# One fused kernel of gated linear attention, mixture of experts and GLU: token numbers in 64-byte lines, less and earlier zeroing, routing cut into four steps

## The chip, the cores and the metric

The kernel runs on one core of a Trainium2 chip. The metric is the device time of one execution in microseconds (us). A core has a matrix engine (PE, TensorE; PEld is its loading of stationary operands), a vector engine (DVE), a scalar engine (ACT), a general engine (POOL, GpSimd) and SP, which here issues most DMAs. Each engine works through its own instructions in order. [...]

## The reference

Three layers follow one another, 3072 tokens (4 batches of 768) of width 384 (8 heads of 48).

```python
# 1. gated linear attention, per batch and head
f = 1 / (1 + exp(-f_logit))
for t in range(768):
    state = f[t][:, None] * state + outer(k[t], v[t])
    y[t] = q[t] @ state
x = y laid out as [3072, 384]
# 2. mixture of 8 experts, each token to its best one
logits = x @ w_gate;  e = argmax(logits);  gate = softmax(logits)[e]
out = gate * sigmoid(x @ w_output_gate)[e] * (relu(x @ w1[e]) @ w2[e])
# 3. gated linear unit, width 1536
result = (sigmoid(out @ wg) * (out @ wv)) @ wo
```

## The kernel before, in words

**The recurrence** takes the tokens in 24 units of 128 (4 batches of 6). A loop over i (lines 711 to 756) is written out in the order in which each engine is to work, with several units in flight. In iteration i, PE forms the scores of unit i (`s_score`, tile pS), then the output of unit i-1 (`s_y`, tile pY), the state's product of unit i (`s_state`, pM), the turned keys of unit i+1 (`s_turn`, pk), the turned output of unit i-1 (`s_rows`, px) and its router logits (`s_logit`, plg). ACT does the exponentials and logarithms (gi, ls, ln) and copies out of PSUM (xT, kt, x); `s_logit` and `s_rows` both need xT, which ACT copies from pY. DVE forms kT, masks the scores (am), makes running sums (ls) and updates the state (sn); POOL forms qT. SP issues the loads of all inputs, in order: ft, qk, v per unit.

**Routing** goes by groups of units; `groups` lists the first unit and the number of units. When the last unit of a group has its logits, a generator `route` is appended, and `step_route` runs its next step once per iteration, behind `s_sum` and ahead of `s_y` (from i = 17 on once more at the end). The lists `first` and `factor` in `choose` hold small instructions of DVE and one each of ACT: `ex` (exponential of the logits, in `first`) and `eg` (exponential of the output gate, in `factor`). `pr` counts on PE how many tokens of each expert come before each token; from it comes the slot `sidx`. Each expert has 512 slots of 386 words in `xs_all` in DRAM: 384 values of a token, its number (stored as 3072 minus the number, so that 0 means none) and its factor. `put_rows` sends a routed unit's rows to their slots: POOL copies the two extra words into the row, and then issues an indirect DMA.

**Zeroing.** Slots that may stay empty are zeroed ahead of the puts: at i = 2 to 9 SP sends 3 blocks of 128 slots per expert (`xs_all<-zrow`, 579 KB each). At i = 16 it zeroes `id_all` (14 KB). The put DMAs wait for the zeroing.

**The experts.** 9 passes follow: expert 0 in two (W0 = 208 tokens and then 288), the other seven by falling count, with 512, 456, 432, 424, 408, 392 and 376 tokens. `gather_rows` loads a pass's rows, `to_xt` turns them, and products with split weights (each weight as a high and a low part, three matmuls for one) go through `mm3`, lines 780 to 782. `feed` loads the weights (SP) and splits them into parts (ACT `w_hi`, DVE `w_lo`), for expert 0 within the recurrence, from i = 5 on one split per iteration. `put_ids` (line 464) writes the numbers of a pass's tokens from the gathered rows to `id_all`, so that the results find their places later. In the same stretch `conv` loads the GLU's weights as 64-bit words into `stg` (POOL's DMA queue, two buffers), and ACT, POOL and DVE turn them into 32-bit floats (`single`, from line 180).

**The GLU** takes 6 groups of 512 tokens; rows go to their places by indirect DMAs with the numbers read from `id_all` (line 971).

A check at the end of the plan compares counts with the sizes laid out; where it fails, a general version runs instead.

## Time and profile before

| what | value |
|---|---|
| median of 3 runs | 879.57 us (876.7 to 880.75) |
| the profiled execution | 882.84 us, of which its span is 881.1 us |
| PE busy | 847.5 us (96%), mean granted clock 0.978 |
| DVE, ACT, POOL busy | 458.5, 350.2, 204.2 us |
| DMA | 88.96 MB in 52750 packets, 12954 of them under 512 B |
| recurrence | about 10 to 158 us of the span |
| passes of the experts | about 158 to 425 us |
| GLU | about 425 to 881 us |

The span is one execution on the core, from its first to its last instruction. PE's busy time holds its slow time too: a matmul at half the clock counts double. So the time that PE lost in a stretch is its idle time and, beside it, the time in which it worked at the lower clock.

### The profile page before, as it was taken

The page shows a single profiled execution, that of the slowest core. Times are in us where ns is not written, and L with a number is a line of the kernel's source. Part 1 is how long each engine was busy: PE and PEld are TensorE (multiplying, and loading weights), DVE is VectorE, ACT ScalarE, POOL GpSimd, SP SyncE. Part 2 cuts the span into 40 slices and gives each one's busy share as a digit, 9 for nine tenths or more (in the row PEclk, how much of TensorE's full clock was granted, in tenths as well). Part 3 has the DMA queues.
Part 4 walks back from the last instruction along what each step waited for, and adds up shares of the span by engine and source line. Part 5 has one row for each costly group of instructions (what it writes and reads, how often), then busy time and mean ns, then how long its engine had stood idle before and what let it go on. Part 6 is the DMA issues. An engine that isn't in the chain of part 4 may idle for free.

```text
span 881.1 us, 14091 instructions
## 1 busy us (share of the span) xinstructions
PE 847.5 (96%) x5388; PEld 752.0 (85%) x5388; DVE 458.5 (52%) x866; ACT 350.2 (40%) x690; POOL 204.2 (23%) x201
## 2 busy tenths in 40 slices
PE   8998889999999999898999999999999999999995
PEld 5887778898899999898888888888888888888885
DVE  7775785557989998788454222222322322232221
ACT  7765674255456546543433212121221221122111
POOL 5215165302544454455200100010010001001001
PEclk9988898999999999999999999999999999999998
DMA  8998462488898988864300110020020001000001
GB/s 194 270 304 255 120 187 70 91 234 218 187 185 206 244 161 230 237 127 62 117 1 1 37 36 1 1 73 1 1 64 8 1 1 37 1 0 36 1 1 39
DMA packets 52750, 88.96 MB, mean 101 GB/s; under 512 B 12954, under 2 KB 33858, under 8 KB 52674
## 3 DMA queue, kind: packets, MB, share of 16 engines
q1 hardware_dynamic: 46050, 64.35, 29.8%
q0 software_dynamic: 6624, 23.62, 9.7%
q8 instruction: 44, 0.72, 0.4%
q14 instruction: 32, 0.26, 0.1%
HBM read 68.35 MB, written 19.60 MB: 100 GB/s over the span
## 4 chain that ended last, share of the span: by engine, by line
issue 49%; PE 23%; DMA 5%; DVE 4%; POOL 2%; ACT 1%; POOLq 0%; ACTq 0%; DVEq 0%
PE po L781 3%; PE ph L780 3%; PE po L780 3%; PE po L782 3%; PE ph L781 3%; PE ph L782 3%; DMA stg<-in_moe_w_out_dram 2%; POOL out_dram L991 2%; DMA stg<-in_moe_w_gate_dram 1%; DMA stg<-in_moe_w_val_dram 1%; DVE w_lo L232 1%; PE ptx L414 1%; PE pY L631 1%; PE pY L639 1%; PE plg L487 1%
## 5 line engine op out<-in xcount | busy, mean ns | idle before, releaser
L1119 DVE TENSOR_TENSOR hf<-pv,sg 128x512 f32<-128x512 f32 x72 | 49.8, 691 | 268.0 <-PE pv L782 264.0
L991 POOL DMA_INDIRECT out_dram<-ob,ids x24 | 23.6, 982 | 404.2 <-DVE ob L990 398.7
L1115 ACT ACTIVATE sg<-pg 128x512 f32<-128x512 f32 x72 | 43.0, 598 | 173.2 <-PE pg L782 173.2
L1122 ACT CAST hh<-hf 128x512 fp32r<-128x512 f32 x72 | 44.7, 621 | 159.5 <-DVE hf L1119 148.3
L232 DVE TENSOR_TENSOR w_lo<-st,w_hi 128x384 fp32r<-128x384 f32 (+1 forms) x112 | 95.5, 882 | 9.1 <-ACT w_hi L231 8.8
L781 PE MATMUL po<-w_lo,hh 128*128 128x384 f32 x288 | 96.6, 335 | 0.0
L780 PE MATMUL po<-w_hi,hh 128*128 128x384 f32 x288 | 96.4, 335 | 0.0
L782 PE MATMUL po<-w_hi,hl 128*128 128x384 f32 x288 | 96.3, 334 | 0.0
L781 PE MATMUL pv<-xt_lo,w_hi 128*128 128x512 f32 x216 | 85.5, 396 | 0.0
L782 PE MATMUL pg<-xt_hi,w_lo 128*128 128x512 f32 x216 | 85.5, 396 | 0.0
L780 PE MATMUL pg<-xt_hi,w_hi 128*128 128x512 f32 x216 | 85.5, 396 | 0.0
L780 PE MATMUL pv<-xt_hi,w_hi 128*128 128x512 f32 x216 | 85.1, 394 | 0.0
L781 PE MATMUL pg<-xt_lo,w_hi 128*128 128x512 f32 x216 | 85.1, 394 | 0.0
L782 PE MATMUL pv<-xt_hi,w_lo 128*128 128x512 f32 x216 | 85.1, 394 | 0.0
L781 PE MATMUL po<-hl,w_hi 128*128 128x208 f32 (+8 forms) x216 | 74.4, 344 | 3.6 <-DVE hl L1042 3.6
L780 PE MATMUL po<-hh,w_hi 128*128 128x208 f32 (+8 forms) x216 | 74.6, 345 | 1.4 <-ACT yt L951 1.4
L1123 DVE TENSOR_TENSOR hl<-hf,hh 128x512 fp32r<-128x512 f32 x72 | 49.9, 693 | 49.4 <-ACT hh L1122 49.4
L782 PE MATMUL po<-hh,w_lo 128*128 128x208 f32 (+8 forms) x216 | 74.3, 344 | 0.0
L780 PE MATMUL ph<-xt_hi,w_hi 128*128 128x288 f32 (+7 forms) x192 | 68.4, 356 | 2.6 <-DVE hl L1042 2.2
L181 POOL TENSOR_SCALAR cva<-cva 128x512 f32<-128x512 f32 (+1 forms) x30 | 57.2, 1907 | 55.6 <-ACT cva L180 55.6
L781 PE MATMUL ph<-xt_lo,w_hi 128*128 128x288 f32 (+7 forms) x192 | 67.5, 352 | 0.1
L782 PE MATMUL ph<-xt_hi,w_lo 128*128 128x288 f32 (+7 forms) x192 | 67.4, 351 | 0.0
(179 smaller groups left out, 1682.5 us busy)
## 6 DMA issues: line engine op xcount, KB each, us to landing
st<-in_moe_w_dram SPq DMA_DIRECT2D x48, 256.0 KB
st<-in_moe_w_dram SPq DMA_DIRECT2D x32, 384.0 KB
qk<-in_qkt_dram SPq DMA_DIRECT2D x48, 192.0 KB
xs_all<-zrow SPq DMA_DIRECT2D x8, 579.0 KB
ft<-in_ft_dram SPq DMA_DIRECT2D x48, 96.0 KB
v<-in_v_dram SPq DMA_DIRECT2D x24, 192.0 KB
stg<-in_moe_w_gate_dram POOLq DMA_DIRECT2D x9, 512.0 KB
stg<-in_moe_w_val_dram POOLq DMA_DIRECT2D x9, 512.0 KB
```

The source lines that it names most:

```text
L181: nc.gpsimd.tensor_scalar(out=af, in0=af, scalar1=HW_LEAST, scalar2=HW_MOST, op0=ALU.max, op1=ALU.min)
L232: nc.vector.tensor_tensor(out=lo, in0=src, in1=hi.bitcast(F32), op=ALU.subtract)
L414: nc.tensor.transpose(pts[kk][:, i * P : i * P + z], rows[0:z, i, kk * P : (kk + 1) * P], ident[0:z, 0:z])
L487: nc.tensor.matmul(pl, lhsT=d["xT"][:, hp, :], rhs=wgp[:, hp, :], start=(hp == 0), stop=(hp == HP - 1))
L780: nc.tensor.matmul(ps, lhsT=ah, rhs=bh, start=first, stop=False)
L781: nc.tensor.matmul(ps, lhsT=ah, rhs=bl, start=False, stop=False)
L782: nc.tensor.matmul(ps, lhsT=al, rhs=bh, start=False, stop=last)
L991: put = nc.gpsimd.indirect_dma_start(out=out[:, :], out_offset=bass.IndirectOffsetOnAxis(ap=idx[g][:, i : i + 1], axis=0), in_=ob, in_offs ...
L1115: nc.scalar.activation(out=sg, in_=pg, func=AF.Sigmoid)
L1119: nc.vector.tensor_tensor(out=hf, in0=pv, in1=sg, op=ALU.mult)
L1122: nc.scalar.copy(hh, hf)
L1123: nc.vector.tensor_tensor(out=hl, in0=hf, in1=hh.bitcast(F32), op=ALU.subtract)
```

## The change

- The rows of `id_all` become 16 words wide. `put_ids` writes the last 16 words of a gathered row (64 bytes: 14 values, the number, the factor) instead of the number alone (4 bytes); the number is then read at word 14. The zeroing of `id_all` goes.
- Slots are zeroed from the 257th of each expert on (it was the 129th): 2 blocks instead of 3, for two experts per iteration at i = 2 to 5. The first weights of expert 0 are issued at i = 6 (it was 3), their splits begin at i = 8 (it was 5). The check asks for 256 tokens of each expert (it was 128).
- `ex` moves from `first` to the head of `factor`. A route now has the steps: `first`; `ex`, product and sum of the output gate; then `pr`, `eg` and the rank; then, for the groups below unit 12, the rest in a step of its own.
- The third and fourth groups are (12, 5) and (17, 5) instead of (12, 6) and (18, 4); EARLY is 17; W0 is 192, so expert 0's passes have 192 and 304 tokens.
- The router's weights are loaded ahead of the first gates' work. In the experts' loop the last route is run to its end at i = 2, and the first step of the plan with it.

```diff
--- before.py
+++ after.py
@@ -63,13 +63,18 @@
     CAPS = (496, 512, 456, 432, 424, 408, 392, 376)
 
     XW = DM + 2
-    EARLY = 18
+
+    IW = 16
+    ID0 = XW - IW
+    EARLY = 17
 
     SOON = 12
 
     LATE = 19
 
-    W0 = 208
+    W0 = 192
+
+    LEAST = 256
 
     PD = P // 2 + D
     NRING = 34
@@ -89,7 +94,8 @@
     x_all = drp.tile([NT, DM], F32, name="x_all")
     xs_all = drp.tile([NSL, XW], F32, name="xs_all")
     yT_all = drp.tile([DM, NT + SLOT], F32, name="yT_all")
-    id_all = drp.tile([NT + SLOT, 1], I32, name="id_all")
+
+    id_all = drp.tile([NT + SLOT, IW], I32, name="id_all")
 
     ident = const.tile([P, P], F32, name="ident")
     tri = const.tile([P, P], F32, name="tri")
@@ -154,13 +160,13 @@
         first = [
             lambda: nc.vector.tensor_reduce(out=m, in_=l, axis=AX.X, op=ALU.max),
             lambda: nc.vector.tensor_tensor(out=t, in0=l, in1=bc(m, NE), op=ALU.subtract),
-            lambda: nc.scalar.activation(out=ex, in_=t, func=AF.Exp),
             lambda: nc.vector.tensor_tensor(out=sc, in0=l, in1=bc(m, NE), op=ALU.is_equal),
             lambda: nc.vector.tensor_tensor(out=sc, in0=sc, in1=e8b, op=ALU.mult),
             lambda: nc.vector.tensor_reduce(out=ms, in_=sc, axis=AX.X, op=ALU.max),
             lambda: nc.vector.tensor_tensor(out=oh, in0=sc, in1=bc(ms, NE), op=ALU.is_equal),
         ]
         factor = [
+            lambda: nc.scalar.activation(out=ex, in_=t, func=AF.Exp),
             lambda: nc.vector.tensor_tensor(out=ohf, in0=oh, in1=g, op=ALU.mult),
             lambda: nc.vector.tensor_reduce(out=sel, in_=ohf, axis=AX.X, op=ALU.add),
             lambda: nc.scalar.activation(out=eg, in_=sel, func=AF.Exp, scale=-1.0),
@@ -311,13 +317,15 @@
         us = slice(u0, u0 + n)
         ms = ms_all[:, us]
         oh, first, factor = choose(rt, lg[:, u0 % (NU // 2) : u0 % (NU // 2) + n, :], u0, n)
-        for f in first:
-            f()
+        def some(todo, most=99):
+            while todo and most:
+                todo.pop(0)()
+                most -= 1
+
+        some(first)
         yield
-        if u0 < SOON:
-            while factor:
-                factor.pop(0)()
-            yield
+        some(factor, 3)
+        yield
         pr = bank_po(MISC, [P, n, NE], "pr")
         nc.tensor.matmul(pr, lhsT=tris, rhs=oh, start=True, stop=False)
         for i in range(n - 1):
@@ -350,10 +358,11 @@
                 ),
                 lambda: nc.vector.tensor_tensor(out=sidx[:, us], in0=pf, in1=ov, op=ALU.add),
             ]
-        while rank or factor:
-            for todo in (rank, factor):
-                if todo:
-                    todo.pop(0)()
+        some(factor, 1)
+        some(rank)
+        if u0 < SOON:
+            yield
+        some(factor)
         if u0 == EARLY:
             nc.vector.tensor_copy(early, carry[:, 0, 0:1])
         ct = rt.tile([P, NE], F32, name="ct", bufs=1)
@@ -446,6 +455,7 @@
                 if p == 0:
 
                     tc.declare_no_dep(get.ins, group="late rows", reason="other rows")
+                    assert len(early_puts) == EARLY
                     for put in early_puts:
                         tc.add_manual_dep(
                             get.ins,
@@ -463,7 +473,7 @@
             r0 = (start[r] if r else s0) + i * P
             nc.sync.dma_start(
                 id_all[bass.ds(r0, n * z), :].rearrange("(b p) o -> p b o", p=z),
-                xs[0:z, i : i + n, DM : DM + 1].bitcast(I32),
+                xs[0:z, i : i + n, ID0:XW].bitcast(I32),
             )
 
     LAST = NU - 1
@@ -672,12 +682,12 @@
             rows_between(nc.vector, fts[3], 30.0)
             load("f", 3)
             load("v", 1)
+            load_router()
             numbers()
             for u in (0, 1):
                 s_log(u)
                 load("f", u + 4)
                 s_sum(u)
-            load_router()
             for u in (0, 1):
                 s_keys(u)
                 s_queries(u)
@@ -697,7 +707,7 @@
             s_state(0)
             constants()
             keep_warm(WARM[1])
-            groups = [(0, 6), (6, 6), (12, 6), (18, 4), (22, 2)]
+            groups = [(0, 6), (6, 6), (12, 5), (17, 5), (22, 2)]
             routing = []
 
             def step_route():
@@ -740,19 +750,16 @@
                     step_route()
                 if i == 1:
                     nc.gpsimd.memset(zrow, 0.0)
-                if 2 <= i < NE + 2:
-
-                    nc.sync.dma_start(
-                        xs_all[(i - 2) * SLOT + P : (i - 1) * SLOT, :].rearrange("(b p) d -> p b d", p=P),
-                        zrow[:, :, 0:XW].to_broadcast([P, NB - 1, XW]),
-                    )
-                if i == 16:
-                    nc.sync.dma_start(
-                        id_all.rearrange("(p c) o -> p (c o)", p=P), zrow[:, 0, 0 : (NT + SLOT) // P].bitcast(I32)
-                    )
-                if i == 3:
+                if 2 <= i < 6:
+
+                    for e in (2 * i - 4, 2 * i - 3):
+                        nc.sync.dma_start(
+                            xs_all[e * SLOT + LEAST : (e + 1) * SLOT, :].rearrange("(b p) d -> p b d", p=P),
+                            zrow[:, :, 0:XW].to_broadcast([P, NB - LEAST // P, XW]),
+                        )
+                if i == 6:
                     feed.issue()
-                if i >= 5:
+                if i >= 8:
                     feed.step(1)
             while feed.left():
                 feed.step()
@@ -937,7 +944,7 @@
             nc.vector.tensor_tensor(out=cnt, in0=cnt, in1=capc, op=ALU.is_le)
             nc.vector.tensor_reduce(out=ok[:, 3:4], in_=cnt, axis=AX.X, op=ALU.min)
             nc.vector.tensor_reduce(out=ok[:, 4:5], in_=fl[:, 0:NE], axis=AX.X, op=ALU.min)
-            nc.vector.tensor_scalar(out=ok[:, 4:5], in0=ok[:, 4:5], scalar1=float(P), scalar2=None, op0=ALU.is_ge)
+            nc.vector.tensor_scalar(out=ok[:, 4:5], in0=ok[:, 4:5], scalar1=float(LEAST), scalar2=None, op0=ALU.is_ge)
             nc.vector.tensor_reduce(out=ok[:, 5:6], in_=ok[:, 0:5], axis=AX.X, op=ALU.min)
             nc.vector.tensor_scalar(out=flag, in0=ok[:, 5:6], scalar1=0.5, scalar2=None, op0=ALU.is_lt)
 
@@ -968,7 +975,9 @@
                 x2 = xsp.tile([P, KD, NB * P], F32, name="x2", tag="xs")
                 ids = ob_.tile([P, NB], I32, name="ids")
                 nc.sync.dma_start(x2, yT_all.rearrange("(k p) n -> p k n", p=P)[:, :, cols])
-                nc.sync.dma_start(ids, id_all[cols, :].rearrange("(b p) o -> p (b o)", p=P))
+                nc.sync.dma_start(
+                    ids, id_all[cols, DM - ID0 : DM - ID0 + 1].rearrange("(b p) o -> p (b o)", p=P)
+                )
                 xg["t", g] = x2
                 idx[g] = ids
 
@@ -1056,10 +1065,13 @@
                     if planning:
                         for _ in range(2):
                             next(planning, None)
-                    elif i > 1 and next(routing, True):
+                    elif i == 2:
+                        for _ in routing:
+                            pass
                         put_rows(6)
                         gather_rows(1)
                         planning = make_plan()
+                        next(planning)
                     if f == PUT_AT and p:
                         put_pass(p - 1)
                     if f == 0 and p:
```

ACT in the recurrence, from the iteration in which the first group's route starts. `ex` and `eg` are the route's two instructions, xT the copy of pY that PE waits for, kt and x the copies behind it, w_hi a split of a weight, gi to ln the work for the next units. Before:

```order
L527 ACTIVATE ln<-ln 112x512
L157 ACTIVATE ex_818<-t_817 128x48
L647 COPY xT<-pY 112x512
L568 COPY kt<-pk 128x448
L480 COPY x<-px 128x384
L231 CAST w_hi<-st_533 128x512
L543 ACTIVATE gi<-ls 112x512
L552 ACTIVATE ls<-ls 112x512
L559 COPY gc_all<-ls 112x4
L526 ACTIVATE ln<-ft_112 112x512
L527 ACTIVATE ln<-ln 112x512
L166 ACTIVATE eg<-sel 128x6
```

The same place after the change:

```order
L657 COPY xT<-pY 112x512
L578 COPY kt<-pk 128x448
L490 COPY x<-px 128x384
L553 ACTIVATE gi<-ls 112x512
L562 ACTIVATE ls<-ls 112x512
L569 COPY gc_all<-ls 112x4
L536 ACTIVATE ln<-ft_112 112x512
L537 ACTIVATE ln<-ln 112x512
L169 ACTIVATE ex_809<-t_808 128x48
L657 COPY xT<-pY 112x512
L578 COPY kt<-pk 128x448
L490 COPY x<-px 128x384
```

`ex` stood one iteration earlier, and `eg` stood where `ex` stands now; `eg` follows one iteration behind it. Both still stand right ahead of an xT, but what they read was made by DVE an iteration before. The split of this iteration's weight is gone to a later one.

SP in the recurrence, from the first zeroing (before) and from the second (after); 128x3x386 and 128x2x386 are the zeroed blocks, st the weights of expert 0. Before:

```order
L745 DMA xs_all<-zrow 128x3x386
L240 DMA st_529<-in_moe_w_dram 128x512
L240 DMA st_531<-in_moe_w_dram 128x512
L240 DMA st_533<-in_moe_w_dram 128x512
L247 DMA st_535<-in_moe_w_dram 128x2x384
L247 DMA st_537<-in_moe_w_dram 128x2x384
L520 DMA qk_116<-in_qkt_dram 48x1024 x2
L520 DMA ft_112<-in_ft_dram 48x512 x2
L516 DMA v<-in_v_dram 128x384
L745 DMA xs_all<-zrow 128x3x386
L520 DMA qk_114<-in_qkt_dram 48x1024 x2
L520 DMA ft_113<-in_ft_dram 48x512 x2
```

After:

```order
L756 DMA xs_all<-zrow 128x2x386 x2
L530 DMA qk_114<-in_qkt_dram 48x1024 x2
L530 DMA ft_113<-in_ft_dram 48x512 x2
L526 DMA v<-in_v_dram 128x384
L756 DMA xs_all<-zrow 128x2x386 x2
L530 DMA qk_115<-in_qkt_dram 48x1024 x2
L530 DMA ft_110<-in_ft_dram 48x512 x2
L526 DMA v<-in_v_dram 128x384
L246 DMA st_764<-in_moe_w_dram 128x512
L246 DMA st_766<-in_moe_w_dram 128x512
L246 DMA st_768<-in_moe_w_dram 128x512
L253 DMA st_770<-in_moe_w_dram 128x2x384
```

Before, the zeroing runs on for six more iterations, each time behind that iteration's loads and ahead of a weight; after, all of it is issued ahead of the first weight.

PE at the end of iteration 18, where the third group's `pr` stands. Before:

```order
L487 MATMUL plg<-wgp,xT 128x16 x4
L578 MATMUL pS<-qT,kT 128x128 x8
L322 LDWEIGHTS tris
L322 MATMUL pr<-oh,tris 128x48
L324 LDWEIGHTS oneb
L324 MATMUL pr<-oh,oneb 128x40
```

After:

```order
L497 MATMUL plg<-wgp,xT 128x16 x4
L330 LDWEIGHTS tris
L330 MATMUL pr<-oh,tris 128x40
L332 LDWEIGHTS oneb
L332 MATMUL pr<-oh,oneb 128x32
```

The counting moved ahead of the next unit's scores, right behind the logits, whose PSUM bank it takes.

## Rows read from the trace of the kernel before

**Rows 1.** Windows over all engines: us, busy time (and count) per engine, PEclk, DMA share, GB/s.

```profile
48.00:52.00 4.00, 2.03 (x12) 2.03 (x12) 2.49 (x9) 2.41 (x6) 0.00 (x0) 0.79 1.05 330
52.00:56.00 4.00, 4.00 (x34) 3.50 (x33) 3.08 (x6) 2.15 (x5) 1.73 (x1) 0.50 1.05 285
56.00:60.00 4.00, 4.00 (x52) 3.62 (x50) 2.38 (x9) 1.98 (x5) 0.00 (x0) 0.86 1.03 268
```

**Rows 2.** PE's timeline: start, duration, instruction, idle time before it and its releaser.

```profile
43.34 0.55 PE L476 MATMUL px<-ident,xT 112*128 112x112 f32 x4
49.97 0.74 PE L476 MATMUL px<-ident,xT 112*128 112x112 f32 x4 [2.17 <-ACT xT L647]
79.07 2.08 PE L578 MATMUL pS<-qT,kT 48*128 48x128 f32 x16 [2.92 <-POOL qT L554]
102.43 0.55 PE L476 MATMUL px<-ident,xT 112*128 112x112 f32 x4
124.03 0.55 PE L476 MATMUL px<-ident,xT 112*128 112x112 f32 x4
151.10 0.60 PE L476 MATMUL px<-ident,xT 112*128 112x112 f32 x4
```

**Rows 3.** ACT's timeline, the two instructions of the first group's route.

```profile
49.20 0.24 ACT L157 ACTIVATE ex<-t 128x48 f32<-128x48 f32 x1 [1.70 <-DVE t L156]
57.09 0.21 ACT L166 ACTIVATE eg<-sel 128x6 f32<-128x6 f32 x1 [2.82 <-DVE sel L165]
```

**Rows 4.** Waits from 0 to 210 us: total us, times, longest.

```profile
ACT eg L166 <- DVE sel L165: 10.2, 5, 2.8
```

**Rows 5.** POOL's timeline, the first put of rows.

```profile
74.94 1.15 POOL L369 DMA_INDIRECT xs_all<-x,sidx  x1 [6.34 <-DVE ls L534]
```

**Rows 6.** SP's timeline, the last zeroing of slots.

```profile
68.04 0.42 SPq L745 DMA_DIRECT2D xs_all<-zrow  x1
```

**Rows 7.** Instructions on the tensor id_all: min/median/max ns, first and last start.

```profile
L464 SPq DMA_DIRECT2D id_all<-xs x17: 319/407/1778, 155.5 to 395.0; - x17
L750 SPq DMA_DIRECT2D id_all<-zrow x1: 423/423/423, 114.5 to 114.5; - x1
```

**Rows 8.** Windows around a writing of numbers, and behind the zeroing of id_all.

```profile
116.00:118.00 2.00, 2.00 (x34) 1.64 (x31) 1.91 (x4) 1.45 (x5) 1.54 (x3) 1.00 0.71 256
...
226.00:228.00 2.00, 2.00 (x10) 1.65 (x9) 1.99 (x4) 0.30 (x2) 0.00 (x0) 1.00 1.66 92
228.00:230.00 2.00, 2.00 (x11) 1.62 (x10) 1.91 (x4) 0.76 (x2) 0.00 (x0) 1.00 0.63 23
...
236.00:238.00 2.00, 2.00 (x11) 1.67 (x10) 1.97 (x4) 1.25 (x3) 0.71 (x2) 1.00 1.04 378
```

**Rows 9.** ACT's timeline, a conversion of the GLU's weights.

```profile
361.93 0.66 ACT L180 ACTIVATE cva<-stg 128x512 f32<-128x512 f32 x1 [4.77 <-DMA stg<-in_moe_w_gate_dram]
```

**Rows 10.** Windows of the last passes.

```profile
360.00:365.00 5.00, 3.64 (x20) 3.09 (x19) 1.74 (x4) 3.07 (x7) 1.91 (x1) 1.00 0.99 368
...
370.00:375.00 5.00, 2.98 (x20) 2.72 (x19) 4.90 (x10) 3.12 (x7) 2.31 (x3) 0.96 0.82 253
375.00:380.00 5.00, 5.00 (x22) 5.00 (x21) 3.64 (x6) 1.12 (x2) 3.27 (x2) 0.70 1.23 128
...
410.00:415.00 5.00, 1.44 (x8) 1.12 (x8) 4.97 (x9) 1.16 (x3) 3.57 (x3) 1.00 0.23 79
415.00:420.00 5.00, 5.00 (x21) 4.83 (x20) 3.04 (x7) 1.28 (x3) 1.61 (x2) 0.66 0.24 68
```

**Rows 11.** Windows of expert 0's first pass, its second, and most of the passes.

```profile
170.00:174.00 4.00, 4.00 (x36) 3.96 (x37) 2.00 (x12) 0.69 (x2) 2.98 (x5) 1.00 0.46 113
...
186.00:196.00 10.00, 10.00 (x79) 10.00 (x78) 7.26 (x14) 8.67 (x19) 0.00 (x0) 1.00 0.88 162
...
200.00:400.00 200.00, 196.44 (x1027) 183.17 (x1027) 175.52 (x279) 111.72 (x227) 94.13 (x76) 0.99 0.86 197
```

## The prediction

> **What bounds the kernel now.** I read the page's slices of PE first: PE is busy nearly everywhere, so time can be had only where PE idles or runs at its lower clock. Windows of 4 us over the recurrence show where. Most are full at clock 1.00; four stretches are not, and [rows 1] show one of them window by window. In the first PE works for 2.03 of 4 us, and then the granted clock falls: 0.79, 0.50, 0.86 in the three windows. The clock's loss is (0.21 + 0.50 + 0.14) x 4 = 3.4 us, beside 2 us of idleness: one such stall costs some 5.4 us. [...]
>
> What they cost together I take from PE's timeline, where px comes once per iteration [rows 2]. Between 102.43 and 124.03 there is no stall: 4 iterations, 5.40 us each. From 43.34 to 151.10 there are 16 iterations and 107.76 us; at 5.40 they would take 86.4. The excess is 21.4 us, which agrees with four stalls of 5.4. Some 1.2 us of it is my estimate for the route's own counting on PE, so 20.2 us can be won. (From here on: the first stall is A, near 50 us, the next B, C and D.)
>
> What released PE in each: in A px waited 2.17 us for ACT's copy xT [rows 2], and ACT had waited 1.70 us for a DVE result just ahead of it, in the route's `ex` [rows 3]. One iteration later `eg` waits 2.82 us in the same way, while the clock is still low. ACT executes in order, so a small instruction that waits for DVE holds up the copy behind it; DVE gets to the route's work late, since it stands behind that iteration's scan. There were five such waits of `eg`, 10.2 us in all [rows 4]. C (px at 93.81) and D (px at 131.84) show the same xT after a late route. B is different: pS waited 2.92 us for POOL's qT [rows 2], and POOL had stood 6.34 us in the first put of rows [rows 5]. The releaser named there, DVE's ls, can't be right for a put; what the put also needs is that the slots are zeroed, and the last zeroing was issued at 68.04 [rows 6], behind a DMA queue that is full from 8 to 76 us (DMA share about 1.05 in each of [rows 1]). So I read B as a wait for the zeroing.
>
> A second place is in the last passes [rows 10]. PE idles 1.36 us in 360 to 365, 2.02 in 370 to 375 and 3.56 in 410 to 415, together 6.9; the clock falls behind the last two: 0.04 x 5 + 0.30 x 5 + 0.34 x 5 = 3.4 us. Together 10.3 us. Ahead of them ACT waited 4.77 us for a piece of the GLU's weights [rows 9]; while it waited, its other work (the activation that feeds the next products, the splits) stood behind. Why was that piece late? Windows of 2 us over the passes show the same event behind every writing of token numbers (there are 17 of these DMAs, [rows 7]): DMA falls from over 240 GB/s to 92, 23 and then 39 and 32, with the DMA engines called busy, and after some 8 us it is back at 378 [rows 8]. Nothing else is issued there at that moment that has tiny packets: each number is a packet of 4 bytes. The zeroing of `id_all` (128 pieces of 112 bytes, issued at 114.5, [rows 7]) is the nearest row for a write of short but longer pieces: DMA moved 256 GB/s in the 2 us behind it [rows 8], no collapse. From 420 us on PE is full and nothing is changed there.
>
> **The change part by part.**
>
> *ex and eg one step later.* The DVE results that they need are then an iteration old (5.4 us), longer than either wait of [rows 3]. That removes what released A and what followed, C and D for the second and third group: three stalls, about 16 us with their clock. What is late next: xT then waits for pY alone, and in stall-free iterations that chain fits into 5.40 us. DVE's work is the same, only its rest (sum, reciprocal, carry) sits in a fourth step; puts of the first group begin one iteration later.
>
> *Zeroing.* 8 x 579 KB becomes 8 x 386 KB, sent in four iterations instead of eight, ahead of expert 0's weights. The last zeroing is issued four iterations earlier (some 20 us), and the first put an iteration later, so the put has about 25 us more than before, against 6.34 missing. B goes: 5.4 us. The price: loads of expert 0's weights come three iterations later, and their 14 splits run from i = 8 to 21 instead of 5 to 18. They are needed only at the first pass, two iterations behind. The bytes asked of the queue by any iteration are no more than before (8 x 386 = 3.1 MB against 4.6 MB), so the inputs of the recurrence should not be late; if they were, the price would be that of a stall, 5.4 us. I take nothing.
>
> So all four stalls: -20.2 us, with the bounds 0 and -21.4.
>
> *pr of the third group behind plg.* It takes the PSUM bank of the logits, so PE must wait for DVE's copy of them. No such wait is in the trace. Above, the nearest row is the idle 2.17 us of [rows 2], which would bring its clock with it (5.4 us); below, nothing, or a gain, since PE no longer counts ahead of `s_y`: -0.4, my estimate of a group's share of the counting. DVE is about a microsecond late in such an iteration by the sum of its work, which is an estimate too; idleness of 1.36 us did not lower the clock (1.00 in the window from 360, [rows 10]). I take +0.8. The last group's does the same at the end of the loop; there it takes the place of idleness that is there before (nothing).
>
> *Three puts of rows at i = 19 and 20, one at i = 21.* Before, three stood at i = 20 and 21. POOL issues as many. A late qT would cost what B cost, 5.4 us; the cover is that qT has had more than an iteration. I take nothing.
>
> *W0.* Pass 0 has 36 products in 4 us, 0.111 us each at 208 columns; pass 1 has 79 in 10 us, 0.127 us at 288 [rows 11]. 0.016 / 80 x 16 columns x 144 products = 0.5 us, won in the one and lost in the other. I take nothing, bounds -1 to +1. The router's earlier load and the first plan step one unit earlier touch no wait of PE that I found: nothing, within the same bounds.
>
> *Lines of 64 bytes.* As many pieces (one per token), 16 times the bytes: 376 to 512 tokens x 64 B is at most 33 KB a pass, nothing beside 378 GB/s. What matters is whether a piece of 64 bytes chokes the DMA as one of 4 does. The bounds are 0 (chokes as much; then the late stalls stay) and -10.3 (all of the late stalls). The nearest row by size is the one with 112 bytes, which did not choke; I take -9.3, leaving a microsecond for work that is late for its own reasons, DVE above all (4.90 and 4.97 of 5 us busy in two of the windows, [rows 10]).
>
> [...]
>
> **The sum**, against the profiled execution: 882.84 - 20.2 + 0.8 - 9.3 = 854.1 us. That execution lies 3.3 us above the median of the runs, 879.57, so I set the forecast at 851 us. If all of the bounds on the good side came: 879.6 - 21.4 - 0.4 - 10.3 - 1 = 846.5.
>
> **The rivals.**
>
> *R1, the lines choke still.* A write of a piece below some size is slow whatever its size, and 64 is nearer to 4 than the 112 of one single DMA shows. For it: the event is bound to small pieces, and the piece count is as before. Against: 256 GB/s at 116 us. Then the recurrence alone is won: 879.6 - 20.2 + 0.8 = 860 us.
>
> *R2, a stall stays or comes up in the recurrence.* The new wait of pr, qT behind three puts, or DVE late for another reason makes PE idle for 2 us or more, and the clock falls behind it. One costs 5.4 us: 856 to 857; two: 862. For it: DVE is the busiest beside PE there (3.0 of 4 us), and a wait removed shows the next one. Against: iterations without a route run at 5.40 us with no idleness worth naming.
>
> *R3, slower than before: the longer lines choke longer.* If a choke's length went by bytes and not by pieces, it would grow beyond 8 us, up to many times. The DMA engines have a share of 0.86 over 200 to 400 us [rows 11], so 28 us of room. There are 8 passes with numbers after that. With the recurrence's 19.4 us won, the change turns slower once 8 x (extra) exceeds 28 + 19.4, that is, when a choke lasts 6 us longer (14 us instead of 8). At twice the length (16 us) it would be 8 x 8 - 28 = +36 us of waiting, -19.4: 896 us. Against it: the 112-byte row again.
>
> *R4, it does not do what it says.* The stalls come from DVE itself, which in these iterations is late by its own load, and not from the place of `ex` and `eg`; xT and masks are then as late as before, and lines of 64 bytes choke as before. Only B goes, and the pr wait costs its upper bound of 5.4: 879.6 - 5.4 + 5.4 = 880 us.
>
> **How the numbers follow.** My forecast 0.56 (its own range 846 to 855); R2 0.20; R1 0.13; R3 0.06; R4 0.05. What a measurement of this kernel can tell from no change is about 0.5%, some 4.4 us. Faster: forecast, R1 and R2, 0.89; same: R4, 0.05; slower: R3, 0.06. The range from 844 to 868 holds the forecast, R1, R2 and a stall beside R1 (866); R3 and R4 are left out, 0.11.
>
> **What would show it.** In the windows of the recurrence PEclk stays at 1.00 from 44 to 150 us, and px comes every 5.4 us to its end; ACT's `ex` and `eg` have no idle time before them; the first put runs without a wait for DMA. Behind each writing of numbers DMA keeps above 200 GB/s, ACT's conversions have no waits of 5 us, and PE is full at 360, 372 and 412 us. I am wrong in the first part if a px or pS waits 2 us or more and the clock falls behind it, and in the second if DMA falls to some 20 to 40 GB/s behind a writing of 64-byte lines.

## The result and the profile after

The changed kernel took 866.9 us (median of 4 runs, 865.4 to 868.1) against 878.3 us of the kernel before beside it: a ratio of 0.987, with an interval from 0.984 to 0.990. Two later sets on other chips gave 867.5 us (0.985, from 0.979 to 0.991) and 863.2 us (0.983, from 0.979 to 0.986). So it is faster, by 1.3 to 1.7%, and by about half as much as forecast: 851 us was 28.6 us below the median it started from, 11 to 16 were measured. The 866.9 us lie at the far end of the stated range of 844 to 868, where a choke with one stall beside it (866) stood; no choke came, so it is luck that the range held the time.

Where the time went is seen by milestones on PE, in the profiled execution of each kernel. Each milestone is the start of an instruction in PE's timeline: px of unit 5, px of unit 22 (the recurrence's end), the first product of expert 0's first pass, the first of the pass with 512 tokens, and the first of the GLU.

| stretch, us in the profiled execution | before | after | change | forecast |
|---|---|---|---|---|
| px of unit 5 to px of unit 22 | 113.7 | 93.0 | -20.6 | -19.4 |
| px of unit 22 to the first pass | 4.4 | 6.1 | +1.7 | 0 |
| expert 0, both passes | 39.7 | 49.3 | +9.6 | 0 |
| pass of 512 tokens to the GLU | 217.8 | 211.1 | -6.7 | -9.3 |
| GLU | 462.1 | 462.2 | 0 | 0 |

Before rounding, the rows sum to -16.1, which is what the spans show (881.1 and 865.0). The profiled execution of before lay 4.6 us above its set's median, 878.3, and that of after at its median: that is the rest up to the -11.4 of the medians.

The recurrence did as forecast. PE's timeline of after: px of unit 5 starts as before, px of unit 21 at 131.08 instead of 151.10 [rows 2].

```profile
43.29 0.55 PE L486 MATMUL px<-ident,xT 112*128 112x112 f32 x4
110.01 0.18 PE L330 MATMUL pr<-oh,tris 128*128 128x40 bf16 x1 [1.19 <-DVE lg L498]
114.59 0.60 PE L576 MATMUL pk<-ident,kT 112*128 112x112 f32 x4 [1.72 <-DVE kT L555]
131.08 0.60 PE L486 MATMUL px<-ident,xT 112*128 112x112 f32 x4
136.30 0.60 PE L486 MATMUL px<-ident,xT 112*128 112x112 f32 x4 [0.69 <-ACT xT L657]
137.98 0.18 PE L330 MATMUL pr<-oh,tris 128*128 128x40 bf16 x1 [0.26 <-DVE lg L498]
141.24 0.85 PE L423 MATMUL ptx<-ident,xs 128*128 128x128 f32 x6 [0.92 <-PE pY L649]
```

Its second and third rows are a new stall of 2.9 us at iteration 18. The last two, pr and ptx, are new waits at the loop's end, 1.2 us together; the 0.69 us ahead of them are not new. The kernel before had those too, and no wait ahead of ptx:

```profile
156.99 0.60 PE L476 MATMUL px<-ident,xT 112*128 112x112 f32 x4 [0.69 <-ACT xT L647]
160.36 0.76 PE L414 MATMUL ptx<-ident,xs 128*128 128x128 f32 x6
```

Behind the waits at the loop's end the clock fell. The windows of after over expert 0's first pass (columns as in [rows 1]; the clock is the one that PE was granted, as a share of full speed) show PE busy throughout, at 0.50, from 142 to 163 us:

```profile
140.00:144.00 4.00, 2.75 (x19) 2.06 (x16) 2.22 (x10) 1.35 (x4) 2.50 (x5) 0.85 0.17 53
144.00:148.00 4.00, 4.00 (x21) 4.00 (x21) 0.53 (x2) 0.81 (x2) 3.17 (x6) 0.50 0.41 149
...
156.00:160.00 4.00, 4.00 (x20) 3.78 (x20) 1.75 (x10) 0.33 (x1) 3.30 (x5) 0.50 0.31 102
160.00:164.00 4.00, 4.00 (x23) 4.00 (x23) 2.04 (x11) 0.33 (x1) 0.00 (x0) 0.59 0.93 298
164.00:168.00 4.00, 4.00 (x38) 4.00 (x38) 0.66 (x4) 0.66 (x2) 0.00 (x0) 1.00 1.06 361
```

PE made 21 matmuls in 4 us instead of 38: busy time hides the loss, the count shows it. Products of this pass start 0.21 us apart at 0.50 and 0.11 us apart at 1.00. Summed over windows of half a microsecond, the low clock took 10.2 us here. In the kernel before, the clock was 1.00 throughout this pass.

Why PE waited ahead of ptx stands in DVE's timeline (the releaser that PE's row names, its own pY, was done at 140.31 us, and ptx started at 141.24). The 14 instructions of the fourth group's last step (first and last shown) come ahead of the scaling of expert 0's rows (L434), which ptx reads:

```profile
138.33 0.20 DVE L341 TENSOR_TENSOR t<-pr,oh 128x40 f32<-128x40 f32 x1 [0.40 <-PE pr L336]
...
140.64 0.17 DVE L370 TENSOR_TENSOR carry<-carry,ct 128x8 bf16<-128x8 bf16 x1
140.72 0.73 DVE L434 TENSOR_SCALAR xs<-xs 128x384 f32<-128x384 f32 x2
```

In the last passes the choke is gone. Numbers were written at 235.51 us, and DMA stays up (compare [rows 8]):

```profile
236.00:238.00 2.00, 2.00 (x11) 1.82 (x10) 2.00 (x3) 1.08 (x3) 1.08 (x2) 1.00 1.02 375
238.00:240.00 2.00, 2.00 (x12) 1.81 (x11) 2.00 (x3) 1.78 (x4) 2.00 (x2) 1.00 0.90 276
```

Of the stalls of 2 us and more in [rows 10] one is left, shorter. It is this wait of PE, with 2.88 us of work in the window from 395:

```profile
398.24 0.44 PE L788 MATMUL po<-hl,w_hi 128*128 128x376 f32 x1 [2.12 <-DVE hl L1051]
```

```profile
395.00:400.00 5.00, 2.88 (x14) 2.56 (x13) 4.93 (x9) 0.30 (x1) 2.56 (x2) 0.88 0.26 79
400.00:405.00 5.00, 5.00 (x22) 4.61 (x21) 2.50 (x5) 1.36 (x3) 1.61 (x2) 0.78 0.36 121
```

### The profile page after: what moved, and what is told of

Read it like the earlier page. It is cut to its first block, busy times and chain, and to the rows that moved or that the text cites. A ratio compares the mean times of both kernels' runs of the same rounds, so it can differ in the third digit from the quotient of the medians.

```text
span 865.0 us, 14074 instructions
## 1 busy us (share of the span) xinstructions
PE 843.2 (97%) x5388; PEld 750.7 (87%) x5388; DVE 463.4 (54%) x866; ACT 351.5 (41%) x690; POOL 211.2 (24%) x201
## 4 chain that ended last, share of the span: by engine, by line
issue 50%; PE 37%; DVE 4%; POOL 3%; DMA 3%; ACT 2%; SPq 0%; POOLq 0%; DVEq 0%; ACTq 0%
PE ph L787 4%; PE ph L788 4%; PE ph L789 4%; PE po L788 4%; PE po L787 4%; PE po L789 4%; POOL out_dram L1000 2%; PE pS L588 2%; PE pY L641 2%; PE plg L497 2%; PE pY L649 2%; DMA st<-in_moe_w_dram 2%; DMA ft<-in_ft_dram 1%; PE ptx L423 1%; PE px L486 1%
## 5 line engine op out<-in xcount | busy, mean ns | idle before, releaser
L788 PE MATMUL po<-hl,w_hi 128*128 128x192 f32 (+8 forms) x216 | 75.7, 350 | 2.1 <-DVE hl L1051 2.1
L787 PE MATMUL po<-hh,w_hi 128*128 128x192 f32 (+8 forms) x216 | 75.7, 350 | 0.0
L789 PE MATMUL po<-hh,w_lo 128*128 128x192 f32 (+8 forms) x216 | 75.5, 350 | 0.0
L187 POOL TENSOR_SCALAR cva<-cva 128x512 f32<-128x512 f32 (+1 forms) x30 | 60.9, 2029 | 47.1 <-ACT cva L186 47.1
L1050 ACT ACTIVATE hh<-ph 128x192 fp32r<-128x192 f32 (+8 forms) x72 | 35.6, 494 | 85.9 <-PE ph L789 85.9
L787 PE MATMUL ph<-xt_hi,w_hi 128*128 128x304 f32 (+7 forms) x192 | 68.0, 354 | 0.9 <-DVE hl L1051 0.5
L237 ACT CAST w_hi<-st 128x384 fp32r<-128x384 f32 (+1 forms) x112 | 59.2, 558 | 20.1 <-PE po L788 20.0
```

Source lines behind the costliest of these rows:

```text
L187: nc.gpsimd.tensor_scalar(out=af, in0=af, scalar1=HW_LEAST, scalar2=HW_MOST, op0=ALU.max, op1=ALU.min)
L237: nc.scalar.copy(hi, src)
L787: nc.tensor.matmul(ps, lhsT=ah, rhs=bh, start=first, stop=False)
L788: nc.tensor.matmul(ps, lhsT=ah, rhs=bl, start=False, stop=False)
L789: nc.tensor.matmul(ps, lhsT=al, rhs=bh, start=False, stop=last)
L1050: nc.scalar.activation(out=hh, in_=pS, func=AF.Relu)
```

## The experiments

The sets ran on different chips, on which the kernel before took 878 to 887 us; so ratios to it are compared, or runs of one set (letters). The ratios have their limit: e11, e12 and e13 are the kernel after but for the token numbers' lines, and took nearly its 211.1 us from the pass of 512 tokens to the GLU, but their ratios are 0.973 to 0.979. So across sets a difference of a per cent tells little. Clocks are the range of each kernel's executions (of before, the profiled one). The last column is what falls of the clock cost in the profiled execution, by half-microsecond windows from 10 to 440 us, with the start of each fall.

| run | set | median us | ratio to before [95%] | clock | us lost to the clock (start) |
|---|---|---|---|---|---|
| before | - | 878.3 | 1 | 0.978 | 3.4 (50), 3.4 (78), 3.4 (95), 3.4 (132), 1.7 (375), 1.7 (416) |
| after | - | 866.9 | 0.987 [0.984, 0.990] | 0.981-0.985 | 10.2 (143), 1.7 (399) |
| e1_warm | A | 863.4 | 0.975 [0.971, 0.979] | 0.987-0.991 | 5.1 (111), 1.7 (142) |
| e2_rank_later | A | 859.9 | 0.970 [0.966, 0.974] | 0.990-0.991 | 1.7 (18), 3.4 (117) |
| e3_w208 | A | 860.7 | 0.971 [0.968, 0.975] | 0.985-0.991 | 5.1 (143) |
| e4_ids4 | A | 876.1 | 0.987 [0.983, 0.992] | 0.981-0.989 | 1.7 each (89, 113, 140, 212, 369), 3.4 (410) |
| after_again | B | 867.5 | 0.985 [0.979, 0.991] | 0.977-0.987 | 3.4 (115), 3.4 (146), 1.7 (395) |
| e5_raise | B | 861.2 | 0.978 [0.972, 0.983] | 0.987-0.991 | 1.7 (110), 1.7 (138), 1.7 (390) |
| e6_only_ids64 | B | 873.0 | 0.990 [0.985, 0.994] | 0.981-0.988 | 3.4 (51), 3.4 (78), 1.7 (95), 1.7 (133), 1.7 (406) |
| e7_old_route | B | 866.7 | 0.983 [0.978, 0.988] | 0.981-0.989 | 3.4 (50), 1.7 (88), 3.4 (118), 1.7 (398) |
| e8_old_zeroing | C | 870.9 | 0.985 [0.980, 0.990] | 0.976-0.981 | 1.7 (81), 5.1 (115), 6.8 (146), 1.7 (402) |
| e9_best | C | 856.8 | 0.969 [0.964, 0.974] | 0.991-0.997 | none |
| e10_best192 | C | 857.6 | 0.969 [0.964, 0.974] | 0.993-0.995 | 1.7 (151), 1.7 (390) |
| e11_ids16B | C | 861.4 | 0.973 [0.967, 0.980] | 0.989-0.991 | 1.7 (112), 1.7 (139), 1.7 (392) |
| e12_ids4_apart | E | 864.0 | 0.979 [0.962, 0.997] | 0.979-0.991 | 1.7 (111), 1.7 (138), 1.7 (391) |
| e13_ids8B | E | 862.2 | 0.977 [0.966, 0.988] | 0.985-0.991 | 1.7 (110), 3.4 (390) |
| e14_best_spread | D | 853.9 | 0.973 [0.970, 0.977] | 0.992-0.995 | 1.7 (62) |
| e9_again | D | 856.0 | 0.975 [0.972, 0.978] | 0.991-0.995 | 3.4 (18), 1.7 (390) |
| after_third | D | 863.2 | 0.983 [0.979, 0.986] | 0.985-0.989 | 1.7 (18), 3.4 (117), 3.4 (148) |

**The yardstick.** The kernel after, unchanged, twice more (after_again, after_third).

> The kernel after, unchanged, as the yardstick on the chip of the other runs of this set. Theory: the same as its first measurement, 865 to 869 us, with a clock of 0.50 through most of expert 0's first pass. Rival (the fall of the clock there is a matter of chance): a clock of 1.00 there and 856 to 858 us.

Neither theory nor rival came out whole: the time is the same, but the profile has the fall in two places. Behind the stall at iteration 18 it runs so:

```profile
112.00:116.00 4.00, 2.46 (x22) 2.43 (x24) 3.96 (x9) 1.69 (x5) 3.28 (x4) 0.89 0.49 129
116.00:120.00 4.00, 4.00 (x38) 3.43 (x38) 3.91 (x8) 2.36 (x5) 3.42 (x4) 0.50 0.49 171
```

In expert 0's first pass it lost 3.4 us instead of 10.2. So the waits at the loop's end are the same in all three profiles (0.69, 0.27 and 0.92 us to a hundredth), and where the clock falls behind them, and for how long, is not.

**The end of the loop.** e1_warm: PE is kept busy there.

```diff
             s_y(NU - 1)
+            keep_warm(5)
             to_xt(0, xg[0], passes[0][2])
```

> The kernel after, with five matmuls of 512 columns that compute nothing needed put on PE between the last pY and the turning of expert 0's first rows (where PE idled 0.92 us, just before its clock fell to 0.50 for 21 us). Theory (the idleness at the loop's end lowers the clock, and the low clock costs 10 us of pass 0): the clock stays at 1.00 from 140 to 163 us and the time falls by about 10 us, to 855 to 858 us. Rival (the clock falls by what pass 0 itself is, with its products of 192 columns): the clock still falls within pass 0, and the time stays at 866 to 868 us.

Inconclusive. The low clock at the pass's start cost only 1.7 us, but in the profile it fell already behind the wait of pr, ahead of the added matmuls, and once more at iteration 18; and e4, e5, e11 and e12, which have no added matmuls there, lost no more than 1.7 us either. 0.975 is 7 to 10 us better than the kernel after by its ratios, but no run of that kernel stands in the same set.

e2_rank_later: the route's last step goes behind the turning.

```diff
-                if i > 16:
+                if 16 < i < NU - 1:
                     step_route()
```

> The kernel after, with the last step of the fourth group's route (pr on PE and 15 small instructions on DVE) moved from the end of iteration 23 behind the turning of expert 0's first rows. Theory (DVE's 15 instructions stand ahead of the scaling of these rows, so PE idles before ptx and the clock falls): the idleness of 0.92 us and pr's wait go, the clock stays at 1.00, time 855 to 858 us. Rival (DVE's place is not the cause): idleness and the fall of the clock remain, time 865 to 868 us.

The waits went as the theory has it: DVE scales the rows ahead of the step's instructions (14, not 15), and PE waits neither ahead of pr nor ahead of ptx. From DVE's and PE's timelines:

```profile
141.87 0.73 DVE L434 TENSOR_SCALAR xs<-xs 128x384 f32<-128x384 f32 x2
145.64 0.19 DVE L341 TENSOR_TENSOR t<-pr,oh 128x40 f32<-128x40 f32 x1
143.70 0.88 PE L423 MATMUL ptx<-ident,xs 128*128 128x128 f32 x6
144.51 0.19 PE L330 MATMUL pr<-oh,tris 128*128 128x40 bf16 x1
```

Since the run differs from the kernel after in this order alone, the place of the step is shown as the cause of these two waits. That the fall of the clock follows from them rests on all of the profiles: of the eleven with the step at the loop's end (the kernel after three times, e1, e3, e4, e5, e8, e11, e12, e13), ten have a fall within 8 us behind px of unit 22, and e13 has none; of the eight without it there, none has. The time alone does not settle it: e3_w208 below, in the same set and with the step unmoved, took 860.7 us against 859.9. What is left in e2's profile are falls at 18 us and at iteration 18.

e3_w208: the widths.

```diff
-    W0 = 192
+    W0 = 208
```

> The kernel after, with W0 = 208 as before, so that expert 0's passes have 208 and 288 tokens. Theory (idleness at the loop's end lowers the clock): the idleness is the same, the clock falls in the same place, time within 2 us of the kernel after (865 to 869 us). Rival (192 columns are the cause of the fall, or of its length): the clock does not fall or is back after some 8 us as in the stalls of the kernel before, time 856 to 862 us.

The waits are the same and the clock fell in the same place (143), so the width is not the cause of the fall. The theory's time was missed: 860.7 us is the rival's. The fall cost 5.1 us, between the 3.4 and 10.2 of the kernel after; whether 208 columns shorten it, these few falls can't tell, and without the kernel after in the same set the time stays unexplained. e10_best192 below has the other half of the answer.

e5_raise: three wide matmuls within the pass.

```diff
+                    if p == 0 and f == 2:
+                        keep_warm(WARM[2])
                     if p == 0 and f == 7:
```

> The kernel after, with three matmuls of 512 columns that compute nothing needed added behind the third unit of expert 0's first pass, within the stretch at clock 0.50; the idleness ahead of the pass is left as it is. Theory (once low, the clock stays low as long as the pass runs with products of 192 columns, and the wide matmuls at the pass's end are what raises it): the clock falls at 142 us as before and is back at 1.00 behind the added matmuls, near 150 us; 6 us less than the kernel after. Rival (the clock comes back after a time of its own, whatever runs): still low until about 163 us, time as the kernel after or 1 us more.

Inconclusive: in its profile the clock fell ahead of the pass (138) and was back before the added matmuls ran. Its median is 6.3 us below that of the kernel after in the same set, as the theory has it, but the one profile does not show the added matmuls as the reason. What ends a low stretch stays open.

**The route's order.** e7_old_route: ex back into `first`, all of `factor` in the second step, rank and `pr` where they stood.

```diff
             lambda: nc.vector.tensor_tensor(out=t, in0=l, in1=bc(m, NE), op=ALU.subtract),
+            lambda: nc.scalar.activation(out=ex, in_=t, func=AF.Exp),
...
-        some(factor, 3)
-        yield
+        if u0 < SOON:
+            some(factor)
+            yield
```

> The kernel after with the route's steps of the kernel before: ex in the first step, eg and the rest in the second, pr of the later groups in the middle of the next iteration. Zeroing, groups, widths and lines of 64 bytes stay as in the kernel after. Theory (ACT's waits for DVE in ex and eg made three of the four stalls): px comes late behind the routes of the three groups, the clock falls behind each, the recurrence is 11 to 16 us longer than in the kernel after; time 10 to 16 us above it, less what a calmer end of the loop gives back (up to 10). Rival (all four stalls came from the zeroing's transfers): no stalls in the recurrence, and the time at or below that of the kernel after.

A, C and D came back, as waits and as falls of the clock, without B. The rows of its PE timeline:

```profile
48.89 0.60 PE L485 MATMUL px<-ident,xT 112*128 112x112 f32 x4 [1.66 <-ACT xT L656]
86.26 0.60 PE L485 MATMUL px<-ident,xT 112*128 112x112 f32 x4 [2.71 <-ACT xT L656]
117.40 0.60 PE L485 MATMUL px<-ident,xT 112*128 112x112 f32 x4 [1.51 <-ACT xT L656]
```

px of unit 22 came at 146.9 us, 8.6 us later than in after_again (138.3), where 11 to 16 were expected. Yet the median was that of the kernel after in the same set (866.7 and 867.5 us). In the two profiles, the loop's end and expert 0 gave back 5.3 of the 8.3 us that the recurrence had lost from px of unit 5 on. This is where most of the gain of the new route went.

**The zeroing.** e8_old_zeroing: `xs_all` is zeroed and the feed started as in the kernel before (both parts of the diff above, undone together).

> The kernel after with the zeroing and the start of the weights' feed of the kernel before (3 blocks per expert at i = 2 to 9, feed from i = 3, splits from i = 5). Theory (POOL's first put waits for the zeroing): the put waits some 5 us, pS waits for qT by 1 to 3 us and the clock falls behind it, near 78 to 90 us; 4 to 7 us above the kernel after. Rival (with the first put one iteration later, the old zeroing is in time): no stall there, time as the kernel after.

B is back, at 2.3 us of waiting, with a fall behind it. PE's row:

```profile
79.22 1.16 PE L588 MATMUL pS<-qT,kT 48*128 48x128 f32 x16 [2.33 <-POOL qT L564]
```

and of POOL's waits in the first 150 us:

```profile
POOL xs_all L378 <- DMA qk<-in_qkt_dram: 5.5, 2, 5.2
```

The put waits 5.2 us for a DMA, though it comes one iteration later, and in the kernel after no put waits more than 0.7 us. The profile names a load as that DMA; that it is the zeroing is inferred from the edit. What it costs is not settled: by the ratios little (0.985 against 0.983 to 0.987); against e11_ids16B of its own set, the kernel after with 16-byte lines, 9.6 us, most of it in longer falls of the clock at 115 and 146 us, which differ between executions of one kernel too.

**The token numbers.** e6_only_ids64 is the kernel before with 64-byte lines alone; e4_ids4 is the kernel after with 4 bytes.

```diff
-    IW = 16
-    ID0 = XW - IW
+    IW = 1
+    ID0 = DM
```

> The kernel before with nothing changed but the token numbers: lines of 64 bytes, and no zeroing of them. Theory (4-byte pieces choke the DMA and so stall the last passes): the four stalls of the recurrence stay; DMA keeps above 200 GB/s behind the writings of numbers where something is asked of it, and the passes from the one of 512 tokens to the GLU's start take 7 to 10 us less than the 217.8 us before; time 7 to 10 us below the kernel before. Rival (the last stalls are DVE's load, whatever the DMA does): 0 to 2 us.

> The kernel after, with the token numbers written as 4 bytes each again. Theory (4-byte pieces choke the DMA, the late weights of the GLU stall PE): DMA falls to 20 to 40 GB/s for some 8 us behind each writing of numbers, waits of 5 us of ACT for the GLU's weights and PE's idleness after 360 us come back, the time rises by 6 us (5 to 10), to 871 to 876 us. Rival (the late stalls went because the recurrence ended earlier): no difference, 866 to 868 us.

e6_only_ids64 is as the theory has it: 9.1 us below the kernel before, with 211.0 us from the pass of 512 tokens to the GLU, where before had 217.8. So is the profile of e4_ids4, with 229.1 there, 18 more than the kernel after. Why the choke cost more there than before is not shown; the profiled execution was the slowest of its four, 4.7 us above their median. By its ratio (0.987) e4_ids4 is no slower than the kernel after in other sets; it is 13 to 16 us slower than the three runs with 64-byte lines in its own set (e1 to e3).

Then the size and the place of a piece: lines of 16 bytes (e11_ids16B) and of 8 (e13_ids8B), and 4 bytes written into a line of 64 each (e12_ids4_apart).

> The kernel after with token numbers in lines of 16 bytes instead of 64. Theory (a piece too short for what the memory takes at once is slow): behind each writing of numbers DMA falls below 100 GB/s for some us, as with 4 bytes, and the passes from 512 tokens to the GLU's start take 217 us or more. Rival (only neighbouring numbers that share one line of memory get in each other's way, and the fewer share, the less): between, 211 to 215 us, with chokes of some 2 us.

> The kernel after with 4 bytes written for each token number, but each into a line of 64 bytes of its own, so that no two numbers share a line. Theory (numbers of different tokens that share a line of memory get in each other's way): no choke, landing within 3 to 5 us of the issue, 209 to 212 us from the pass of 512 tokens to the GLU's start. Rival (a piece of 4 bytes is slow in itself, wherever it goes): DMA at 20 to 100 GB/s for some 8 us behind each writing, 217 to 229 us there.

> The kernel after with the token numbers in lines of 8 bytes, packed. Theory (sharing): more neighbours share a line than with 16 bytes (8 instead of 4), half as many as with 4 bytes; a choke of about half the length, 211 to 216 us from the pass of 512 tokens to the GLU's start. Rival (a piece of 4 bytes is a case of its own): as with 16 bytes, 211 us.

The stretch took 211.3, 211.1 and 212.9 us (two runs each). The windows some 5 to 10 us behind the same writing, first e4_ids4, then e12_ids4_apart, then e13_ids8B:

```profile
241.00:243.00 2.00, 2.00 (x12) 1.82 (x11) 1.90 (x5) 1.06 (x2) 0.17 (x1) 1.00 0.95 45
243.00:245.00 2.00, 2.00 (x17) 1.68 (x15) 2.00 (x3) 0.62 (x1) 1.09 (x2) 1.00 0.49 29
```

```profile
233.00:235.00 2.00, 2.00 (x12) 1.82 (x11) 1.90 (x5) 1.06 (x2) 0.02 (x1) 1.00 0.72 210
235.00:237.00 2.00, 2.00 (x16) 1.69 (x15) 2.00 (x3) 1.32 (x3) 1.25 (x2) 1.00 0.50 184
```

```profile
233.00:235.00 2.00, 2.00 (x11) 1.83 (x10) 1.90 (x4) 1.07 (x2) 0.00 (x0) 1.00 0.86 74
235.00:237.00 2.00, 2.00 (x17) 1.68 (x15) 2.00 (x3) 1.66 (x4) 1.59 (x2) 1.00 0.80 220
```

Behind the next writing, 8 bytes and 16 bytes (e13_ids8B, then e11_ids16B):

```profile
242.00:244.00 2.00, 2.00 (x12) 1.82 (x11) 1.93 (x4) 0.58 (x2) 0.25 (x1) 1.00 0.87 63
242.00:244.00 2.00, 2.00 (x12) 1.82 (x11) 1.87 (x5) 0.55 (x2) 0.00 (x0) 1.00 0.96 147
```

In these windows a piece of 4 bytes alone in its line does not choke (210 and 184 GB/s), packed 4-byte ones do (45 and 29), packed 8-byte ones for 2 to 4 us (74 and 63), and packed 16-byte ones slow DMA slightly and for a shorter time (147 at a share of 0.96). Counted by windows of 1 us, up to 12 us behind the writings from 170 us on, a DMA share over 0.4 with less than 100 GB/s stood for 53 us in e4_ids4, 29 in e13_ids8B, 17 in e11_ids16B, 10 in e12_ids4_apart, 9 in the kernel after. So in these runs it is not the length of a piece alone, but how many short ones lie side by side. Why neighbours hurt, and whether by a line of memory that they share, as the theories of e12_ids4_apart and e13_ids8B have it, is not shown.

**The mended order.** e9_best: both late countings back where they stood, W0 = 208; e10_best192 the same with 192.

```diff
-                if i > 16:
+                if i in (17, NU - 2):
                     step_route()
```

> The kernel after with W0 = 208 and with both late countings (pr) where the kernel before had them: for the third group in the middle of iteration 19 instead of at the end of 18, for the fourth behind the turning of expert 0's first rows. ex and eg stay one step behind, zeroing and 64-byte lines as in the kernel after. Theory (idleness of 2 us and more within a few us lowers the clock, at iteration 18 by the wait of pr and a late kT, and at the loop's end): no fall of the clock between 100 and 165 us, 8 to 10 us below the kernel after, 25 us or more below the kernel before (ratio 0.965 to 0.972). Rival (DVE's late work at iteration 19 makes the stall there anew, as D in the kernel before): one fall of 3.4 us stays; ratio 0.972 to 0.978.

> The same with W0 = 192. Theory (the width matters little where the clock is up): within 1.5 us of the run with 208. Rival (passes of 192 columns run at the lower clock in themselves): a low clock in expert 0's first pass, 5 to 10 us above the run with 208.

The theory held: no fall in the profile of e9_best, and the first pass at full clock:

```profile
136.00:140.00 4.00, 3.82 (x51) 3.18 (x48) 1.85 (x8) 1.45 (x5) 0.00 (x0) 1.00 0.03 3
140.00:144.00 4.00, 4.00 (x39) 4.00 (x38) 3.00 (x20) 1.38 (x5) 1.38 (x3) 1.00 0.02 4
```

The width made no difference where the clock is up (856.8 and 857.6 us). e9_best's profile is of its fastest execution; e9_again's has falls at 18 and 390 us, and none between 100 and 165 either. e10_best192 has one in expert 0's first pass, at 151 us, behind a wait of the plan's product pf. e9_best has the same wait of 1.40 us, with no fall behind it. From e10_best192:

```profile
148.74 0.20 PE L884 MATMUL pf<-chk,onec 128*1 128x10 f32 x2 [1.40 <-DVE chk L881]
```

In set D, e9_again took 856.0 us against 863.2 of the kernel after: 7.2 us from the order of two steps (and W0, which counted 0.8 us in set C). The granted clocks leave no overlap: 0.977 to 0.989 in the twelve executions of the kernel after, 0.991 to 0.997 in the thirteen of e9_best, e9_again and e10_best192. The kernel before had 0.974 to 0.986 in the sets' runs, so the kernel after won idle time and little of the clock.

e14_best_spread adds one more: the parts of the GLU's first tokens one third at a time.

```diff
                         if f == 5:
-                            tok_parts(0)
+                            parts0 = tok_parts(0)
+                        if f >= 5:
+                            parts0(1)
```

> The ninth kernel (late countings where the kernel before had them, W0 = 208) with the parts of the GLU's first tokens made one third each behind units 5, 6 and 7 of the last pass, instead of all behind unit 5. Theory (what is left of the late stalls is these three DVE instructions, 2.2 us, ahead of hl, and not the DMA): the wait of po for hl (2.1 us) and the fall of the clock that follows in some executions go, 2 to 4 us below the ninth kernel. Rival (DVE is simply full there): the wait moves one unit on, no difference.

po's wait for hl fell from 2.1 to 0.6 us:

```profile
387.32 0.44 PE L788 MATMUL po<-hl,w_hi 128*128 128x376 f32 x1 [0.60 <-DVE hl L1057]
```

The stretch fell from 211.0 to 207.9, about half of it by a fall of the clock that e9_again had there and e9_best (209.6) had not. At 853.9 us against 856.0 and 863.2 it has the lowest median here. The late rest was for the most part DVE's order, not the DMA.

The shift of groups to (12, 5) and (17, 5), the router's earlier load and the earlier plan were not run apart.

## Why the prediction was wrong

**The four stalls, -20.2: right**, cause by cause. The recurrence gained 20.6 with pr's 2.2 us (below) in it, so the stalls' part was some 22.8; e7_old_route brought A, C and D back, e8_old_zeroing B. In the kernel before, px of C and of D had waited for xT as A's had, and each of the four falls, A to D, cost 3.4 us (table):

```profile
93.81 0.60 PE L476 MATMUL px<-ident,xT 112*128 112x112 f32 x4 [2.95 <-ACT xT L647]
131.84 0.69 PE L476 MATMUL px<-ident,xT 112*128 112x112 f32 x4 [2.53 <-ACT xT L647]
```

One premise was wrong without harm: in four iterations the zeroing now asks for 772 KB instead of 579, not for less, and qT waited 3.1 us for a load where it had waited 2.3.

**pr behind plg, +0.8: too small.** It was 2.9 us of idleness (1.19 for lg, 1.72 for a late kT behind the route's small DVE instructions and a weight's split), 2.2 us over the step of 5.40, and 3.4 more in the two later profiles, where the clock fell. The wait was foreseen; what DVE had queued behind it was not.

**"The last group's does the same at the end of the loop; there it takes the place of idleness that is there before (nothing)": the step that failed.** It took no idleness's place: the 0.69 us that were there before stayed. The step moved 14 DVE instructions ahead of the scaling that ptx waits for. That stretch became 1.7 us longer, 1.2 of it new waits, and a fall of the clock behind them cost 10.2 us in expert 0's passes in the first profile, 3.4 in the two later ones. I looked at what the moved matmuls wait for, and not at what their readers on DVE stand ahead of. R2 named the kind, a new wait of pr and the clock behind it, and its case of two stalls (862 us) is what came; but it priced one at 5.4 us, from the falls of 3.4 us that the trace of before had. How long the fall would be was not to be foreseen from that trace.

**Lines of 64 bytes, -9.3: the mechanism right, the size -6.7 in the profiles** (9.1 by the medians of e6_only_ids64, which has this change alone). The choke went; of the stall at 410 in [rows 10], 3.56 us, of which I had given all but a microsecond to the DMA, 2.12 us stayed, and e14_best_spread shows that these were for the most part three DVE instructions ahead of hl. R1 fell: behind one writing 64-byte pieces ran free (375 and 276 GB/s), lone 4-byte ones too (210 and 184), and packed 16-byte ones nearly so (low flow for 17 us in all, against 9 with 64 bytes).

**W0 and the later weights, 0: right as far as shown.** e10_best192 is within 0.8 us of e9_best, and PE has no wait for an early weight; e3_w208 leaves open whether 192 columns lengthen a fall. The plan's earlier step, put at nothing, does show where the clock is up: pf waits 1.0 us for DVE in the two later profiles of the kernel after, 0.58 in the kernel before.

**The base.** The forecast priced the late stalls and all four falls from a profiled execution 4.6 us above its set's median, and took 3.3 off the level, nothing off the terms.

## What to carry to other kernels

A step that is moved takes its readers along: list what the engine that reads its result has queued behind them, and who waits for that. Where the clock falls behind idleness of PE, as here, give a new wait a price with a wide range, since the falls seen so far need not be the longest (3.4 us each in the recurrence before, then 10.2), and look at the count of matmuls (21 instead of 38 in 4 us), since busy time doesn't show it. Where many short pieces choke the DMA, as the packed 4-byte numbers did, spread them or make them longer: the low flow fell from 53 us to 10 with each in a line of its own, and to 9 with 64 bytes. Fewer pieces were not tried.

## What the hardware showed

The same waits gave falls of different length: behind the loop's end of the kernel after the clock cost 10.2, 3.4 and 3.4 us in three profiled executions, and behind the same three waits (0.69, 0.26, 0.92 us) in e13_ids8B it did not fall. PE's rows, and the window behind them:

```profile
136.04 0.60 PE L486 MATMUL px<-ident,xT 112*128 112x112 f32 x4 [0.69 <-ACT xT L657]
137.72 0.18 PE L330 MATMUL pr<-oh,tris 128*128 128x40 bf16 x1 [0.26 <-DVE lg L498]
140.97 0.85 PE L423 MATMUL ptx<-ident,xs 128*128 128x128 f32 x6 [0.92 <-PE pY L649]
142.00:146.00 4.00, 3.86 (x33) 3.69 (x33) 1.42 (x5) 1.28 (x5) 3.16 (x7) 1.00 0.39 138
```

The length of a wait does not tell either: in e14_best_spread the clock fell at 62 us behind waits of 0.40 and 0.26 us, while 1.36 us at 362 in [rows 10] brought no fall. So the 2 us that R2 and e9_best's theory name are no threshold. Behind packed writes of 4 bytes DMA fell as low as 23 GB/s and was back after some 8 us [rows 8]; behind the same pieces 64 bytes apart it ran at 210 and 184 (e12_ids4_apart).
